# Turning a convolution filter to step-major: transposing DMAs and a DRAM bounce in place of identity matmuls

## The chip, the cores and the metric

The kernel runs on one core of one Trainium2 chip. The metric is the device time of one execution in microseconds (us); the time of a version is the median over its runs.

The core has a matmul engine (TensorE; PE in the profile, its weight loads PEld), a vector engine (VectorE, DVE), an activation engine (ScalarE, ACT), a general one (GpSimd, POOL) and a synchronizing one (SyncE, SP) that here issues nearly all loads. Each engine works through its own instructions in program order and waits for the others by semaphores. Transfers run on 16 DMA engines that all queues share.

## The reference, cut to what matters

```python
xn = layernorm(q)                                   # (1, 2048, 640)
# A: gated long convolution, channel by channel
k_shift = sum over t of k_pad[:, t:t+S, :] * shift_k[:, 3-t]    # 4 taps
kv  = k_shift * v
kv_f = rfft(kv padded to 2S);  kf_f = rfft(ssm_k padded to 2S)  # ssm_k: (640, 2048)
y   = irfft(kv_f * kf_f)[:2048] + kv * ssm_D
s   = xn * y
# B: a dense layer pair on the same xn
g   = silu(gelu(xn @ w1 + b1) @ w2 + b2)            # 640 -> 1728 -> 640
out = q + s * g
```

S is 2048 steps, D is 640 channels. All tensors are bfloat16. The filter `ssm_k` comes channel-major, one row of 2048 steps for each of 640 channels, while k, v and q come step-major.

## The kernel before, in words

The convolution is a discrete Fourier transform in two stages of matmuls. A step s is written as s = 16 p + n, with p one of 128 partitions and n one of 16. The first stage multiplies, for each n, a 128 x 640 slab (128 values of p by 640 channels) with two 128 x 128 matrices, WA and WB. For the signal these are the steps `uf`, for the filter the steps `kf`. The results are cast out of PSUM (`ue`, `ke`) and written to DRAM scratch (`us` to scrU, `ks` to scrK); they are read back in another order (`ml`, `fl`) and go through a second stage with small matrices (`mu`, `ff`). The filter's spectrum stays in the tile Khat; the signal's is multiplied with it (`mp`), and two inverse stages (`mc`, `y`) with another bounce through scrC give y. The dense pair B (`h` for the first layer, `g` for the second) works on four chunks of 512 steps, and its matmuls are laid between those of the convolution.

The order of all work is written out by hand: PLAN is a string of steps, and each step issues its instructions on the engines that it uses, so the order of steps is the order on each engine's queue. A suffix .a or .d says whether ACT or DVE does an evacuation.

The part that concerns us is how the filter gets from channel-major to the slabs that `kf` reads:

- `C0` to `C4` (load_kf, line 198, SP's queue) load 128 channels by 2048 steps each into the first 16 rows of Khat, seen as `kf_sb` (partition = channel within a tile of 128).
- `d` (add_d, line 498, DVE) adds ssm_D to step 0. This makes the skip term kv * ssm_D a part of the filter. ssm_D comes with the bias rows in `prm` (`P2`), is turned with them (`pt`, `pb`) and lies in `dD_sb` with the channel on the partition.
- `kt0` to `kt15` (k_tr, line 424, PE) turn, for each n, five 128 x 128 blocks by matmuls with the identity into one PSUM tile; `kc0` to `kc15` (k_tr_out, line 427, on ACT or DVE by the suffix, printed as L135 and L136) copy it to a row tile kT.
- `kf0` to `kf31` (k_f1, line 430 by way of mm2 at line 340, PE) multiply kT with WA and WB.

PSUM has three tiles of the kind "big" in turn; kt, kf, uf and the other convolution stages all use them. There are two row tiles for kT. The shifted and gated signal is made by `cv` steps on DVE; the step cv7 of the first pair of n multiplies with v's first quarter (`V0`), cv23 with the second (`V1`). Each `X` loads a chunk of q, each `K` a quarter of k. On POOL the queue holds the stores `ks`, `us`, `ms` and the small power `lr` (ln_root, line 359), which the normalization steps `ln` on DVE wait for.

Of the kernel before, what the change touches and what calls it, by code (L numbers as in the profile page):

```python
# [11 lines left out]
BF16 = mybir.dt.bfloat16  # L12
I32 = mybir.dt.int32
ACT = mybir.ActivationFunctionType
ALU = mybir.AluOpType

P = 128
S = 2048
D = 640
F = 1728  # L20
NJ = 16
DT = D // P
FT = (F + P - 1) // P
# [9 lines left out]
X1 ls4 ls5 ls7 ls6 lv1 C0 X3 cv17 cv18 g0 ge0 gm0 g1 ge1 gm1 ws0 cv19 g2 ge2 g3 ge3 g4 cv20 cv21 cv22 ws1 g5 lr1  # L33
ln7 ln5 ws2 C4 C3 C1 V0 cv7 cv15 C2 d kt0 kc0.a kt1 kc1.a kf0 kf1 ke0.a kt2 kc2.a V1 ln4 kf2 ke2.a cv24 cv23 X2
cv25 ke1.d ks0 gm2 ge4 ln6 kf3 ke3.d ks1 kf4 ke4.a gm4 ge5 kt3 kc3.d kf5 ke5.a ks2 V2 tt7 te7.a kt5 kc5.d tt9
te9.a kt4 gm5 kf7 cv26 cv27 cv28 kf6 kc4.a ke6.a ke7.a ks3 g6 ge6 kf8 ke8.a kf9 ke9.d ks4 kf10 ke10.a K2 tt8
te8.a kt6 kc6.d kf11 ke11.a ks5 kt9 kc9.d gm3 kf12 ke12.a tt5 te5.d tt6 te6.a uf1 kt7 kf13 kc7.a ke13.a ks6 g7
ge7 ls12 uf0 ue0.a ue1.d us0 cv29 cv30 cv31 V3 h14 he14 kf14 ke14.d kf15 ke15.d ks7 h15 he15 kt8 kc8.d kf19 kf18
ke18.a ke19.d ks9 kt10 kc10.a cv32 cv33 cv34 cv35 cv36 kf16 ke16.a kt12 cv40 kf17 kc12.a ke17.a ks8 h16 he16 uf3
uf2 ue2.a ue3.a us1 h17 he17 kf21 kf20 ke20.a ke21.d ks10 kt11 kc11.a h18 he18 uf5 uf4 ue4.a ue5.d us2 kf22  # L40
ke22.d ls10 h19 he19 kt14 kf24 ke24.d sm kf23 kc14.a ke23.a ks11 h20 he20 kf25 ke25.d ks12 kt13 kc13.d kf28
ke28.a h21 he21 uf6 ue6.a kf29 ke29.a ks14 uf7 ue7.a us3 h22 he22 h23 he23 kf26 ke26.a gm7 cv37 cv38 cv41 cv42
cv39 kf27 ke27.a ks13 kt15 kc15.d kf30 ke30.a kf31 ke31.a ks15 fl0 fl1 fl2 h24 he24 fl4 uf10 ue10.a gm6 ls15 ls8
ls9 uf8 ue8.a ls14 uf11 ue11.a us5 h25 he25 h26 he26 uf14 ue14.a cv43 ls13 lv3 lr3 h27 he27 cv44 ls11 lv2 lr2
cv45 cv46 cv47 uf12 ue12.a uf9 ue9.a us4 fl3 uf15 ue15.a us7 g8 ge8 gm8 ln13 ln9 uf13 ue13.a us6 fl5 g9 ge9 ff3
fe3.a ln12 ff1 fe1.d ln10 ff2 fe2.a cv56 ff0 fe0.a cv48 cv49 cv50 ln8 uf21 uf20 ue20.a ue21.a us10 ff8 fe8.a
ln11 g10 ge10 uf16 ue16.a ff6 fe6.d gm9 ff9 fe9.a fl7 ff5 fe5.a ff7 fe7.a fl9 ff4 fe4.a fl8 uf17 ue17.a us8 g11
ge11 cv51 cv52 cv53 cv54 cv55 ff11 fe11.a ff10 fe10.a fl6 uf18 ue18.d uf19 ue19.a us9 fl11 uf26 ue26.a cv57 cv58
cv59 uf24 ue24.a uf27 ue27.a us13 uf25 ue25.a us12 fl12 ff16 fe16.d ff17 fe17.a fl15 ff12 fe12.a tt12 te12.a
ff14 fe14.a cv60 cv61 cv62 cv63 ff18 fe18.a ff15 fe15.a fl13 g12 ff19 fe19.a fl10 uf22 ue22.d ff13 fe13.a fl14  # L50
uf31 gm11 ge12 uf30 ue30.a ue31.d us15 ff23 fe23.d gm12 uf23 ue23.a us11 gm10 tt14 te14.d uf29 uf28 ue28.d
ue29.a us14 mk0 ml0 ml1 mk1 mk2 mk3 ml2 ml3 ml5 ml4 ff31 fe31.a tt13 te13.a tt10 te10.d it0 ie0.d ff27 fe27.d
ff25 fe25.d g13 ge13 gm13 g14 ge14 gm14 ff29 fe29.d ln14 ff28 fe28.a ff24 fe24.d g15 ge15 gm15 ff21 fe21.a tt11
te11.d ff22 fe22.a mu0 mp0 ff26 fe26.a ml7 h28 he28 mu2 mp2 ml10 ml8 mu1 mp1 mk4 mc0 me0.a h29 he29 ff30 fe30.a
mu3 mp3 mk5 ml12 h30 he30 ml11 mc2 me2.a mu4 mp4 mc1 me1.a ms0 mu5 mp5 mk6 h31 he31 ml6 ff20 fe20.a mc3 me3.a
ms1 ln15 mu6 mp6 mc4 me4.a mu7 mp7 mk7 ml9 h32 he32 mu8 mp8 mc5 me5.a ms2 mc6 me6.a mu11 mp11 mc7 me7.a ms3 mu10
mp10 h33 he33 mu9 mp9 mk8 mk9 mc8 me8.a mc10 me10.a mu12 mp12 mu13 mp13 mk10 mc11 me11.a ms5 ml14 h34 he34 ml15
mc12 me12.a it1 ie1.d mc13 me13.a ms6 mu15 mp15 h35 he35 mu14 mp14 mk11 ml13 mc9 me9.a ms4 mu18 mp18 h36 he36
mc14 me14.a mu17 mp17 h37 he37 mu16 mp16 mk12 mc15 me15.a mu20 mp20 h38 he38 mu19 mp19 mk13 mc18 me18.a h39 he39
mu21 mp21 mk14 mc16 me16.a tt17 mc19 me19.a ms9 mc17 me17.a ms8 mu23 mp23 mc20 me20.a mu22 mp22 mk15 h40 he40  # L60
mc21 me21.a ms10 mu24 mp24 mu25 mp25 mc22 me22.a h41 he41 te17.d mc24 me24.a mu26 mp26 mc25 me25.a ms12 tt15
te15.a mu27 mp27 tt16 te16.d mc23 me23.a ms11 mc26 me26.a tt18 te18.d mu29 mp29 it3 ie3.a mu28 mp28 g16 ge16
gm16 mc27 me27.a ms13 it2 ie2.d tt19 te19.a mu31 mp31 mu30 mp30 ms7 q0 g17 ge17 gm17 mc28 me28.a mc31 mc29
me29.d ms14 mc30 me30.d me31.d ms15 yl5 yl2 yl0 yl4 yl3 yl1 yl6 yl11 yl15 q1 g18 ge18 gm18 g19 ge19 gm19 g20
ge20 gm20 g21 ge21 gm21 g22 ge22 gm22 g23 ge23 gm23 h42 he42 h43 he43 y0 yt0 yo0 h44 he44 h45 he45 h46 he46 y5
yt5 yl8 y4 yt4 yo4 yo5 ys2 y1 yt1 yo1 ys0 y3 yt3 h47 he47 h48 he48 h49 he49 h50 he50 h51 he51 y2 yt2 yl7 yl14
yl9 yl10 yl12 yo2 yo3 ys1 q2 h52 he52 h53 he53 h54 he54 h55 he55 y6 yt6 yl13 yo6 y7 yt7 yo7 ys3 q3 y8 yt8 yo8
y11 yt11 g24 ge24 g25 ge25 g26 y12 yt12 gm24 ge26 gm25 ga24 ga25 gs25 y15 yt15 g27 ge27 y14 yt14 y13 yt13 gm26
ga26 gm27 ga27 gs27 y9 yt9 yo9 ys4 y10 yt10 yo10 yo11 ys5 g28 ge28 gm28 ga28 g29 ge29 gm29 ga29 g30 ge30 gm30
ga30 gs30 g31 ge31 gm31 ga31 gs29 gs31  # L70
# [4 lines left out]
def kernel(  # L75
# [15 lines left out]
    nc = tc.nc  # L91
# [4 lines left out]
    NG = 32  # L96
# [7 lines left out]
    consts = ctx.enter_context(tc.tile_pool(name="consts", bufs=1))  # L104
    wts = ctx.enter_context(tc.tile_pool(name="wts", bufs=1))
    dram = ctx.enter_context(tc.tile_pool(name="dram", bufs=1, space=bass.MemoryType.DRAM))
# [11 lines left out]
    scrU = dram.tile([P * 32, D], BF16, name="scrU")  # L118
    scrC = dram.tile([P * 32, D], BF16, name="scrC")
# [13 lines left out]
    def evac(eng, out_ap, in_ap):  # L133
        if eng == "a":
            return nc.scalar.copy(out=out_ap, in_=in_ap)  # L135
        return nc.vector.tensor_copy(out=out_ap, in_=in_ap)  # L136
# [4 lines left out]
    Khat = wts.tile([P, NG + NR, D], BF16, name="Khat")  # L141
    skp = consts.tile([P, DT, 4], BF16, name="skp")
    prm = consts.tile([FT + DT, P], BF16, name="prm")
    b1_f = consts.tile([P, FT], F32, name="b1_f")
    dD_sb = consts.tile([P, DT], BF16, name="dD_sb")
    ident = consts.tile([P, P], BF16, name="ident")
# [5 lines left out]
    WA = consts.tile([P, NJ, P], BF16, name="WA")  # L152
# [28 lines left out]
    kf_sb = Khat[:, 0:NG // 2, :].rearrange("p g d -> p (g d)").rearrange("p (t j) -> p t j", t=DT)  # L181
    kf_v = kf_sb.rearrange("p t (a b) -> p t b a", b=NJ)

    def load_params(i):
        with nc.allow_non_contiguous_dma(reason="tiny parameter loads"):
            if i == 0:
                nc.sync.dma_start(out=prm[0:FT - 1, :], in_=B_b1[0:(FT - 1) * P].rearrange("(t p) -> t p", p=P))
            elif i == 1:
                nc.sync.dma_start(out=prm[FT - 1:FT, 0:FLAST], in_=B_b1[(FT - 1) * P:F].rearrange("(o p) -> o p", o=1))
            else:  # L190
                nc.sync.dma_start(out=prm[FT:FT + DT, :], in_=A_ssm_D.rearrange("(t p) -> t p", p=P))
# [4 lines left out]

    def load_kf(t):
        nc.sync.dma_start(out=kf_sb[:, t, :], in_=A_ssm_k[t * P:(t + 1) * P, :])
# [47 lines left out]
    sm = {}  # L246
# [68 lines left out]
    live = {}  # L315
# [7 lines left out]
    def big_of(key, bf=False):  # L323
        return take(key, ps_big, [P, 1024] if bf else [P, 2, 512], BF16 if bf else F32, "big")
# [4 lines left out]
    def row_of(key):  # L329
        return take(key, ep, [P, D], BF16, "row", NROW)  # L330
# [7 lines left out]
    def mm2(ps, lhsT, rhs, start=True, stop=True):  # L338
        for h in range(2):
            nc.tensor.matmul(out=ps[:, h, 0:HALF], lhsT=lhsT, rhs=rhs[:, h * HALF:(h + 1) * HALF], start=start, stop=stop)  # L340
# [80 lines left out]
    def k_tr(n2):  # L421
        tp = big_of(("kt", n2), True)
        for t in range(DT):
            nc.tensor.transpose(out=tp[:, t * P:(t + 1) * P], in_=kf_v[:, t, n2, :], identity=ident[:])

    def k_tr_out(n2, eng):
        evac(eng, row_of(("kT", n2))[:], live["kt", n2][:, 0:D])

    def k_f1(i):
        mm2(big_of(("kf", i)), (WA, WB)[i % 2][:, i // 2, :], live["kT", i // 2])  # L430
# [66 lines left out]
    def add_d():  # L497
        nc.vector.tensor_tensor(out=kf_sb[:, :, 0], in0=kf_sb[:, :, 0], in1=dD_sb[:], op=ALU.add)
# [7 lines left out]
    def param_tr():  # L506
        pt = big_of(("pt", 0), True)
        nc.tensor.transpose(out=pt[:, 0:FT + DT], in_=prm[:, :], identity=ident[0:FT + DT, 0:FT + DT])

    def param_out():  # L510
        pt = live["pt", 0]
        nc.vector.tensor_copy(out=b1_f[:], in_=pt[:, 0:FT])
        nc.vector.tensor_copy(out=dD_sb[:], in_=pt[:, FT:FT + DT])
# [59 lines left out]
    def prologue():  # L573
# [90 lines left out]
        "P": load_params, "pt": param_tr, "pb": param_out, "X": load_x, "A": load_w1, "B": load_w2, "C": load_kf, "K": load_k, "V": load_v,  # L664
# [4 lines left out]
        "kt": k_tr, "kc": k_tr_out, "kf": k_f1, "ke": k_f1_out, "ks": k_store,  # L669
# [40 lines left out]
```

## Time and profile before

| | |
|---|---|
| runs | 229.15, 231.75, 233.93 us; median 231.75 |
| the profiled execution, its span | 231.0 us |
| instructions | 3921 |
| DMA | 57.61 MB, mean 249 GB/s; HBM read 33.76 MB, written 18.35 MB |
| `kt` matmuls | 80, first at 42.7, last at 76.7 us |
| loads of ssm_k | 5 of 512 KB, issued from 16.0 to 24.9 us, landing 8.8 to 13.7 us later |
| stores to scrK | 16 of 320 KB, landing after 2.6 us (median) |
| loads from scrK | 16 of 320 KB, 4.6 us |

The profile is of one execution. Its span is 0.75 us below the median of the runs. Its page gives each engine's busy time and then the span in 40 slices of 5.8 us, where a digit is the busy share in tenths; PEclk is the clock granted to TensorE, DMA the mean busy share of the 16 DMA engines, GB/s what they moved. A listing by time has start, length, engine, line and operation, with "out<-in" by the names of the program, and in brackets the idle time before it and what ended it. "SPq" lines are DMA issues on SP's queue. For a DMA issue the last number is the time from issue to landing.

### The profile page before, as it was taken

The numbers are of one execution on the slowest core, as the hardware profiler recorded it, in microseconds if no ns is written. First come the engines' busy times: TensorE is split into PE (matmuls) and PEld (weight loads), VectorE is DVE, ScalarE is ACT, GpSimd is POOL, SyncE is SP. The second block draws the span as 40 slices with busy tenths as digits, with TensorE's granted clock in tenths as the row PEclk, the third lists the DMA queues.
The fourth block names the chain that finished last, engine by engine and source line by source line (L and its number), as shares of the span: only waits on it lengthen the run. The fifth ranks groups of instructions, "written<-read, shape, count | busy, mean of one in ns | idle before, by whom it ended". The sixth has DMA issues, their size and how long they took to land.

```text
span 231.0 us, 3921 instructions
## 1 busy us (share of the span) xinstructions
PE 211.6 (92%) x1420; PEld 131.7 (57%) x1420; DVE 184.1 (80%) x315; ACT 149.6 (65%) x232; POOL 43.1 (19%) x75
## 2 busy tenths in 40 slices
PE   7859999899999899979999965999999999999993
PEld 4524456677555556646765532556677765457772
DVE  7799999889989999999779885699998115444892
ACT  3934687998988999898468742567782244562111
POOL 8100020042232344120200220212222000100010
PEclk9988999999999999999999997999999999999999
DMA  7999995654844479599779999877943695379323
GB/s 219 349 380 355 409 413 206 191 209 174 305 191 188 179 236 381 176 309 337 266 215 294 303 353 295 257 231 188 270 156 131 207 340 200 150 218 367 124 89 114
DMA packets 25209, 57.61 MB, mean 249 GB/s; under 512 B 2854, under 2 KB 14055, under 8 KB 25190
## 3 DMA queue, kind: packets, MB, share of 16 engines
q1 hardware_dynamic: 20726, 39.66, 52.6%
q0 software_dynamic: 4320, 17.70, 20.5%
q8 instruction: 11, 0.18, 0.3%
q14 instruction: 8, 0.07, 0.1%
q10 hardware_dynamic: 144, 0.01, 0.0%
HBM read 33.76 MB, written 18.35 MB: 226 GB/s over the span
## 4 chain that ended last, share of the span: by engine, by line
PE 65%; ACT 12%; DMA 9%; DVE 8%; issue 3%; SPq 1%; DVEq 0%; ACTq 0%
PE g L399 22%; PE h L380 21%; ACT Khat L135 6%; DMA kh<-scrU 6%; PE uf L340 3%; PE mc L537 3%; DMA Khat<-Khat 3%; PE mc L538 2%; PE mu L340 2%; PE kf L340 2%; PE ff L340 2%; PE y L556 2%; PE y L557 2%; DMA skp<-in_A_shift_k_dram 1%; ACT sl L404 1%
## 5 line engine op out<-in xcount | busy, mean ns | idle before, releaser
L380 PE MATMUL h<-xnT,w_sb 128*128 128x512 bf16 x280 | 68.4, 390 | 1.5 <-ACT hT L386 1.2
L399 PE MATMUL g<-w_sb,hT 128*128 128x320 bf16 x448 | 63.7, 299 | 0.6 <-ACT sl L404 0.6
L386 ACT ACTIVATE hT<-h,b_f 128x512 bf16<-128x512 f32 (+1 forms) x56 | 38.3, 690 | 27.3 <-PE h L380 24.2
L399 PEld LDWEIGHTS <-hT 128*128 128x128 bf16 x448 | 43.8, 98 | 18.1 <-issue 0.8
L529 DVE TENSOR_TENSOR p<-mu,Khat 128x1280 bf16<-128x1280 f32 x32 | 45.8, 1484 | 5.4 <-PE mu L340 3.7
L380 PEld LDWEIGHTS <-w_sb 128*128 128x128 bf16 x280 | 27.9, 100 | 31.3 <-issue 4.6
L404 ACT ACTIVATE sl<-g 128x320 bf16<-128x320 f32 x32 | 13.9, 439 | 36.1 <-PE g L399 32.5
L135 ACT CAST c<-mc 128x640 bf16<-128x640 f32 x29 | 19.9, 692 | 8.6 <-PE mc L538 7.9
L544 POOL DMA_DIRECT2D scrC<-c x16 | 11.5, 718 | 56.0 <-ACT c L135 51.8
L409 DVE TENSOR_TENSOR xn<-xn,sl 128x320 bf16<-128x320 bf16 x32 | 10.1, 322 | 14.0 <-ACT sl L404 13.8
L472 DVE TENSOR_TENSOR uc<-uc,kvtmp 128x1280 bf16<-128x1280 bf16 x24 | 19.8, 824 | 0.7
L476 DVE TENSOR_TENSOR kvtmp<-kh,w_exp 128x1280 bf16<-128x1280 bf16 x24 | 19.7, 820 | 0.5
L340 PEld LDWEIGHTS <-mats 128*128 128x128 bf16 x128 | 12.1, 97 | 13.8 <-issue 4.9
L537 PE MATMUL mc<-p,mats 128*128 128x320 bf16 x64 | 18.6, 305 | 1.2 <-DVE p L529 0.7
L538 PE MATMUL mc<-p,mats 128*128 128x320 bf16 x64 | 18.5, 304 | 0.0
L563 DVE TENSOR_TENSOR t<-y,xn 128x640 bf16<-128x640 f32 x12 | 9.8, 820 | 10.4 <-PE y L557 10.3
L135 ACT CAST Khat<-uf 128x640 bf16<-128x640 f32 x26 | 17.0, 697 | 0.4 <-PE uf L340 0.4
L340 PE MATMUL mu<-kh,mats 128*128 128x320 bf16 x64 | 13.5, 300 | 3.7 <-DMA kh<-scrU 2.5
L135 ACT CAST Khat<-ff 128x640 bf16<-128x640 f32 x24 | 15.5, 699 | 0.5 <-PE ff L340 0.4
L135 ACT CAST Khat<-kf 128x640 bf16<-128x640 f32 x22 | 15.1, 711 | 0.3 <-PE kf L340 0.2
L440 POOL DMA_DIRECT2D scrK<-Khat x16 | 8.9, 554 | 31.2 <-ACT Khat L135 16.6
L340 PE MATMUL ff<-kin,mats 128*128 128x320 bf16 x64 | 12.3, 298 | 1.4 <-ACT Khat L135 1.3
(111 smaller groups left out, 269.4 us busy)
## 6 DMA issues: line engine op xcount, KB each, us to landing
scrK<-Khat POOLq DMA_DIRECT2D x16, 320.0 KB, 2.6
scrU<-Khat POOLq DMA_DIRECT2D x16, 320.0 KB, 4.2
kin<-scrK SPq DMA_DIRECT2D x16, 320.0 KB, 4.6
Khat<-Khat SPq DMA_DIRECT2D x32, 160.0 KB, 4.2
kh<-scrU SPq DMA_DIRECT2D x16, 320.0 KB, 5.4
scrC<-c POOLq DMA_DIRECT2D x16, 320.0 KB, 3.9
kh<-scrC SPq DMA_DIRECT2D x16, 320.0 KB, 6.2
kh<-in_A_k_dram SPq DMA_DIRECT2D x4, 640.0 KB, 6.1
```

What stands on the lines that cost most here:

```text
L135: return nc.scalar.copy(out=out_ap, in_=in_ap)
L340: nc.tensor.matmul(out=ps[:, h, 0:HALF], lhsT=lhsT, rhs=rhs[:, h * HALF:(h + 1) * HALF], start=start, stop=stop)
L380: nc.tensor.matmul(out=ps[:, :], lhsT=w1_sb[:, t, ft * P:(ft + 1) * P], rhs=xnT[:, t, :], start=(t == 0), stop=(t == DT - 1))
L386: nc.scalar.activation(out=hT[0:M, ft, :], in_=live["h", i][0:M, :], func=ACT.Gelu_apprx_tanh, bias=b1_f[0:M, ft:ft + 1], scale=1.0)
L399: nc.tensor.matmul(out=ps[:, 0:HALF], lhsT=hT[0:M, ft, q * P:(q + 1) * P], rhs=w2_sb[0:M, ft, hs], start=(ft == 0), stop=(ft == FT - 1))
L404: nc.scalar.activation(out=sl[:], in_=live["g", i][:, 0:HALF], func=ACT.Silu)
L472: nc.vector.tensor_tensor(out=uc[:], in0=uc[:], in1=kvtmp[:], op=ALU.add)
L476: nc.vector.tensor_tensor(out=(kvtmp if s else uc)[:], in0=kh[:, r0:r0 + KC, :], in1=w_exp[:, j:j + 1, :].to_broadcast([P, KC, D]), op=ALU ...
L529: nc.vector.tensor_tensor(out=p[:].rearrange("p k (h c) -> p k h c", h=2), in0=live["mu", g][:, None, :, 0:HALF].to_broadcast([P, 2, 2, HA ...
L537: nc.tensor.matmul(out=psC[:, h, 0:HALF], lhsT=I1a, rhs=p[:, 0, hs], start=True, stop=False)
L538: nc.tensor.matmul(out=psC[:, h, 0:HALF], lhsT=I1b, rhs=p[:, 1, hs], start=False, stop=True)
L544: nc.gpsimd.dma_start(out=pair_view(scrC)[g2], in_=live["c", g2][:])
```

## The change

The filter is turned by the DMA engines. Four transposing loads (`C0` to `C3`) each read 512 steps of all 640 channels from DRAM and write them to four rows of Khat with the step within a block of 128 on the partition: Khat[q, j] holds step 128 j + q. That is step-major, but with the step split as 128 j + q and not as 16 p + n. So four stores (`cb0` to `cb3`, POOL's queue) write these rows to a DRAM scratch scrT in the order of steps, and four loads (`cl0` to `cl3`, SP's queue, 32 partitions each) read it back as s = 16 p + n into the same rows of Khat. `kf` then reads Khat in place of kT; the steps `kt` and `kc` are gone. ssm_D is loaded as a row of 640 (`P2`), and `d` adds it to partition 0 of Khat's row 0; dD_sb and its five rows of prm are gone.

```diff
+    scrT = dram.tile([S, D], BF16, name="scrT")
...
-    prm = consts.tile([FT + DT, P], BF16, name="prm")
+    prm = consts.tile([FT, P], BF16, name="prm")
-    dD_sb = consts.tile([P, DT], BF16, name="dD_sb")
...
-    kf_sb = Khat[:, 0:NG // 2, :].rearrange("p g d -> p (g d)").rearrange("p (t j) -> p t j", t=DT)
-    kf_v = kf_sb.rearrange("p t (a b) -> p t b a", b=NJ)
+    def turn_k(i):
+        nc.sync.dma_start_transpose(out=Khat[:, 4 * i:4 * i + 4, :], in_=A_ssm_k[:, 4 * i * P:4 * (i + 1) * P])
+
+    def bounce_k(i):
+        nc.gpsimd.dma_start(out=scrT.rearrange("(j q) d -> q j d", q=P)[:, 4 * i:4 * i + 4, :], in_=Khat[:, 4 * i:4 * i + 4, :])
+
+    def load_kT(i):
+        a, b = i * 32, i * 32 + 32
+        nc.sync.dma_start(out=Khat[a:b, 0:NJ, :], in_=scrT.rearrange("(p n) d -> p n d", n=NJ)[a:b])
...
-                nc.sync.dma_start(out=prm[FT:FT + DT, :], in_=A_ssm_D.rearrange("(t p) -> t p", p=P))
+                nc.sync.dma_start(out=row_of(("D", 0))[0:1, :], in_=A_ssm_D.rearrange("(o d) -> o d", o=1))
...
-    def load_kf(t):
-        nc.sync.dma_start(out=kf_sb[:, t, :], in_=A_ssm_k[t * P:(t + 1) * P, :])
...
-    def k_tr(n2):
-        tp = big_of(("kt", n2), True)
-        for t in range(DT):
-            nc.tensor.transpose(out=tp[:, t * P:(t + 1) * P], in_=kf_v[:, t, n2, :], identity=ident[:])
-
-    def k_tr_out(n2, eng):
-        evac(eng, row_of(("kT", n2))[:], live["kt", n2][:, 0:D])
-
     def k_f1(i):
-        mm2(big_of(("kf", i)), (WA, WB)[i % 2][:, i // 2, :], live["kT", i // 2])
+        mm2(big_of(("kf", i)), (WA, WB)[i % 2][:, i // 2, :], Khat[:, i // 2, :])
...
     def add_d():
-        nc.vector.tensor_tensor(out=kf_sb[:, :, 0], in0=kf_sb[:, :, 0], in1=dD_sb[:], op=ALU.add)
+        row = Khat[0:1, 0, :]
+        nc.vector.tensor_tensor(out=row, in0=row, in1=live["D", 0][0:1, :], op=ALU.add)
...
     def param_tr():
         pt = big_of(("pt", 0), True)
-        nc.tensor.transpose(out=pt[:, 0:FT + DT], in_=prm[:, :], identity=ident[0:FT + DT, 0:FT + DT])
+        nc.tensor.transpose(out=pt[:, 0:FT], in_=prm[:, :], identity=ident[0:FT, 0:FT])
...
     def param_out():
         pt = live["pt", 0]
         nc.vector.tensor_copy(out=b1_f[:], in_=pt[:, 0:FT])
-        nc.vector.tensor_copy(out=dD_sb[:], in_=pt[:, FT:FT + DT])
```

In PLAN the order around the filter's loads becomes this, and apart from it only the `kt` and `kc` steps are taken out:

```text
before: K1 cv16 X1 ls4 ls5 ls7 ls6 lv1 C0 X3 cv17 cv18 g0 ... g4 cv20 cv21 cv22 ws1 g5 lr1 ln7 ln5 ws2
        C4 C3 C1 V0 cv7 cv15 C2 d kt0 kc0.a kt1 kc1.a kf0 kf1 ke0.a kt2 kc2.a V1 ln4 kf2 ke2.a cv24 cv23 X2 cv25 ke1.d
after:  K1 cv16 X1 ls4 C0 cb0 ls5 ls7 ls6 lv1 X3 C1 cb1 C2 cb2 C3 cb3 cv17 cv18 g0 ... g4 cv20 cv21 cv22 ws1 g5 lr1
        cl0 cl1 ln7 ln5 ws2 V0 cl2 cl3 cv7 cv15 d kf0 kf1 ke0.a V1 ln4 kf2 ke2.a cv24 cv23 X2 cv25 ke1.d
```

## The prediction

> **What bounds the kernel now.** I read the page's head first, then the stretches of six microseconds, then the instructions of each engine in order of time around the filter work, then the DMA issues.
>
> ```profile
> PE 211.6 (92%) x1420; PEld 131.7 (57%) x1420; DVE 184.1 (80%) x315; ACT 149.6 (65%) x232; POOL 43.1 (19%) x75
> ...
> DMA  7999995654844479599779999877943695379323
> GB/s 219 349 380 355 409 413 206 191 209 174 305 191 188 179 236 381 176 309 337 266 215 294 303 353 295 257 231 188 270 156 131 207 340 200 150 218 367 124 89 114
> ```
>
> TensorE is busy in 92% of the span and its program is one fixed order, so a wait at one place moves all that follows. The DMA engines are full in the first six slices (35 us), idle right after, and never full for long again. The filter lies at that seam:
>
> ```profile
> 16.00:17.00 1.00, 0.95 (x3) 0.39 (x3) 1.00 (x3) 0.58 (x1) 0.00 (x0) 0.50 1.07 362
> ...
> 30.00:36.00 6.00, 5.36 (x38) 3.61 (x37) 5.51 (x15) 5.55 (x8) 1.55 (x1) 1.00 1.03 415
> 36.00:42.00 6.00, 6.00 (x46) 4.30 (x44) 5.90 (x11) 4.50 (x5) 0.00 (x0) 1.00 0.27 108
> 42.00:48.00 6.00, 5.11 (x51) 3.91 (x49) 4.67 (x9) 5.99 (x10) 1.17 (x2) 1.00 0.81 250
> ...
> 84.00:90.00 6.00, 5.71 (x43) 3.97 (x42) 5.86 (x13) 5.84 (x10) 4.63 (x5) 1.00 1.02 352
> ```
>
> Columns: stretch and length, busy time of PE, PEld, DVE, ACT, POOL, then granted clock, DMA share and GB/s. At 30 to 36 full DMA engines move 415 GB/s; from 36 to 42 they are nearly free while PE, DVE and ACT are full. From 42 on ACT is the fullest.
>
> ```profile
> 35.08 7.78 PE L399 MATMUL g<-w_sb,hT 128*128 128x320 bf16 x56 [0.64 <-ACT sl L404]
> 42.70 0.78 PE L424 MATMUL kt<-ident,Khat 128*128 128x128 bf16 x10
> 44.08 0.43 PE L340 MATMUL kf<-kT,WA 128*128 128x320 bf16 x2 [0.60 <-ACT kT L135]
> ```
>
> TensorE reaches the filter at 42.7 us and the first kf runs at 44.1. All it needs from DRAM landed some 5 us before: the filter costs no wait today. The inputs come by SP's queue in this order:
>
> ```profile
> 15.51 0.43 SPq L168 DMA_DIRECT2D xn<-in_A_q_dram  x1
> 15.98 0.43 SPq L198 DMA_DIRECT2D Khat<-in_A_ssm_k_dram  x1
> 16.46 0.43 SPq L168 DMA_DIRECT2D xn<-in_A_q_dram  x1
> 16.93 6.94 SPq L198 DMA_DIRECT2D Khat<-in_A_ssm_k_dram  x3
> 23.91 0.43 SPq L179 DMA_DIRECT2D vc<-in_A_v_dram  x1
> ...
> xn<-in_A_q_dram SPq DMA_DIRECT2D x1, 640.0 KB, 11.0
> ```
>
> The last line is the issue at 15.51 (chunk 1 of x, X1): it landed at 15.51 + 11.0 = 26.5. Issued behind it in the same queue, the filter's bytes move after 26.5 in both kernels.
>
> **What is removed.** 80 transposes and 16 copies.
>
> ```profile
> L135 ACT COPY kT<-kt x9: 672/693/785, 43.4 to 70.2; 128x640 bf16<-128x640 bf16 x9
> L136 DVE COPY kT<-kt x7: 481/492/492, 47.2 to 77.1; 128x640 bf16<-128x640 bf16 x7
> ...
> 59.96 0.31 PE kt L424 x5
> ```
>
> In the chain of waits (start, length, what) five transposes take 0.31, so PE loses 16 x 0.31 = 5.0 us; ACT 9 x 0.69 = 6.2; DVE 7 x 0.45 (0.49 less overlap) = 3.1. In the six stretches from 42 to 78 the busy sums are PE 33.9, ACT 33.8, DVE 32.7 of 36; afterwards 28.9, 27.6, 29.6. No engine can then need less than 29.6, so the gain is at most 6.4, at least some 3 if waits between the engines stay; I take 5.0, PE's own share. Edits in the parameter transpose and add_d (0.15 to 0.2 us each) count nothing: they lie beside DVE's wait, below.
>
> **What is added: a chain of DMAs in front of the first kf.** The filter is 2048 x 640 x 2 = 2.62 MB. Before, it was moved once; now three times (turned in, written out, read back), and each pass must be complete before the last starts: every kf reads all 128 partitions, which come by four loads, and each load overwrites rows of Khat that all four stores still read. Step by step:
>
> 1. *Four transposing loads, 0.655 MB each.* No row shows one. Lower bound: 415 GB/s, 1.6 us. Upper: pieces of 256 bytes (128 columns), 10240 in all, each at a price per packet from the page's two big queues (20726 packets of 1913 bytes at 93.8 ns, 4320 of 4097 bytes at 175 ns, by share times 16 engines times span): 37 ps per byte plus 23 ns, so 32 ns, over 16 engines 20.6 us, 5.2 each. Nearest row: reading runs of 1024 bytes is like the loads from scrK with 1280-byte rows, 352 GB/s at 84 to 90, hence 1.9; I take 2.4 for the finer writing. The Trainium skill (DMA: Bandwidth & Descriptors, Latency and other measured facts) has one measured DMA transpose at 261 GB/s, which would be 2.5 us each and 0.4 us more in all; no run shows it yet.
> 2. *The stores (cb), 0.655 MB each, on POOL's queue.* cb0 to cb2 run beside the later transposes but on the same engines: 1.6 each. So C0 lands at 26.5 + 2.4 = 28.9, X3 (1.6) at 30.5, C1 at 30.5 + 2.4 + 1.6 = 34.5, C2 38.5, C3 42.5. cb3 is exposed: issue 0.55 (the scrK stores' 0.54), landing 2.6 for 320 KB plus 0.8 for the second half: 46.45.
> 3. *The loads (cl) with V0 among them.* A lone 640 KB load of v took 4.2 us at the least, 1.6 of them bytes: 2.6 fixed. V0 1.6. The four loads fill 32 partitions each: at full rate 6.4; at that of the stretch below, where the swaps between partition halves are in flight and full DMA engines (1.04) move only 250 GB/s, 10.5. So 10.6 to 14.7, near neither; 12.5. Last load at 59.0.
>
> ```profile
> 120.00:124.00 4.00, 4.00 (x24) 2.25 (x23) 3.60 (x3) 3.97 (x7) 0.00 (x0) 1.00 1.04 250
> ```
>
> First kf at 59.0 instead of 44.1: 14.9 later, PE idle from 42.7. Nothing covers this: everything behind kf0 on PE waits with it. After such an idle time the granted clock falls: at 16 to 19 us, after PE's gaps from 13.5, it is 0.50 for 3.4 us. That costs up to 1.7; I take 1.5. PE's sum: 14.9 + 1.5 - 5.0 = +11.4.
>
> *Who else waits.* POOL's stores stand ahead of ln_root for chunk 1 (lr1), which waits until C3 lands: 42.5 + 0.55 + 1.55 = 44.6 instead of 34.8; DVE's ln7, ln5 wait with it, but DVE's next, cv7, needs V0, now at some 53, so that is hidden. SP's V1 stands behind the four loads: 59.0 + 1.6 = 60.6. DVE's cv23, which uses it, ran at 42.3: 18.3 later, and ke1 and the kf buffers queue behind it. Of this DVE recovers its idle time (36 - 32.7 = 3.3) and its copies (3.1): 18.3 - 6.4 = +11.9. X2, V2 and K2 are needed well after.
>
> The larger of the two, 11.9, moves the end: everything after 84 us waits only for engines or for DMAs that this chain itself feeds, so nothing takes it back. 231.0 + 11.9 = 242.9 for the span of the profiled execution; the median of the runs stands 0.3% above that span (231.75), so **243.7**.
>
> **Bounds.** Least: after 26.5, 4 transposes, X3, 4 stores, 4 loads and V0 are 9.2 MB; at 415 GB/s 22.1 us, plus some 3 for the two hand-overs: 51.6, 7.5 late; less 6.4, plus 1: +2.1, some 234. Most: 5.2 per transpose (C3 at 53.7, cb3 at 57.7) and loads at 14.7: 72.4, 28.3 late, less 3, plus 1.7: +27, some 259.
>
> **Rivals.**
> - *Faster (0.04).* The place is the wait of the first kf on the last load; if the filter is there by 42.7, PE's 5.0 is pure gain, 226.7. It pays from readiness before 44.5, since 2% is 4.6 us. For: the DMA engines idle from 36 to 42. Against: 9.2 MB in a dependent chain from 26.5 gives 51.6 even at the best rate in the page.
> - *No change within 2% (0.13).* The chain runs near the best rate and the removed work returns 6.4: 233.5 to 236.4. For: full DMA engines do hold 415 GB/s for 6 us. Against: the half-partition slices, and that stores and transposes share engines.
> - *A dear transpose (0.18).* By pieces of 256 bytes, with slow loads: 251 to 259. For: the packet fit; against: it prices reading runs that are four times as long.
> - *Tiles one after another (0.05).* If the 80 blocks of 128 x 128 (32.8 KB) went through one after another, each at one engine's rate (415 / 16 = 26 GB/s, 1.26 us), the transposes would take 101 us, C3 would land at 129, the last load at 145, and with +101 late, +1.5, -5 the sum would be some 329. No transfer in the trace is confined so, nor is any a transpose. The Trainium skill (VectorE: DVE Perf Modes, The three transpose paths) gives 1309 ns for a 128 x 128 block by DMA against 390 on TensorE and advises TensorE where its output may go to PSUM; here the trace has a TensorE block at 62 ns in a row.
> - *Not a turning DMA at all (0.02).* If it became copies of single elements, 1.31 million pieces at 23 ns over 16 engines are 1.9 ms.
> - *My forecast (0.58):* 237 to 251.
>
> **How the numbers follow.** A measurement of this kernel tells about 2% from no change. Faster 0.04; within 2% 0.13 (227.1 to 236.4); slower the rest, 0.83. The range 234 to 256 leaves out the faster case (0.04), the last two rivals (0.07) and the ends of the unchanged (0.02) and the dear one (0.07), 0.2 together.
>
> **What would show it.** Khat's transposing issues landing 2 to 3 us apart from 29 on, the last at 42 or so; stores to scrT ending near 46; the four loads ending near 59; PE idle from 42.7 until then with its first kf at a granted clock of 0.5; DVE idle before its product with vc; no kt group; and the order of work after the first kf a little denser than before. I am wrong if the first kf starts before 51 (the chain is cheaper than its bytes), if PE finds other work in the gap, if a later wait gives back the delay, or if a single transpose takes over 5 us.

## The result and the profile after

| | before | after |
|---|---|---|
| runs, median (range) | 230.89 us (229.15 to 233.93, 4 runs) | 257.92 us (255.40 to 258.62, 4 runs) |
| ratio of after to before, 95% interval | | 1.1185, 1.1081 to 1.1289 |
| profiled execution, its span | 231.0 us | 255.3 us |
| DMA moved; packets, of these under 512 bytes | 57.61 MB; 25209, 2854 | 62.83 MB; 35615, 13261 |

The kernel before has one run more here (230.04) than in the table ahead of the prediction. Some executions of a kernel are 1 to 2% longer than others without any change; the ratios leave these out, the medians and the spans do not.

The changed kernel is slower by 12%: 24.3 us of span. The head of its page:

```profile
PE 209.2 (82%) x1340; PEld 126.7 (50%) x1340; DVE 181.1 (71%) x307; ACT 144.3 (57%) x223; POOL 45.4 (18%) x79
...
PEclk9979999555579999999999999979999999999999
DMA  6999999589963855696995899979693469359422
GB/s 218 365 376 343 180 303 321 184 179 257 334 252 150 298 205 205 207 344 221 306 328 194 234 334 317 346 207 304 166 275 149 156 216 368 125 183 347 165 77 103
```

TensorE is busy for 2.4 us less in all (211.6 before), although its span is 24 us longer: time was added in which it does nothing. The seam that the forecast looked at, in stretches of six microseconds (stretch and length, busy time of PE, PEld, DVE, ACT, POOL, granted clock, DMA share, GB/s):

```profile
36.00:42.00 6.00, 6.00 (x46) 4.29 (x45) 2.55 (x4) 4.50 (x5) 1.52 (x2) 1.00 1.13 270
42.00:48.00 6.00, 0.48 (x4) 0.11 (x2) 0.80 (x2) 1.07 (x1) 1.82 (x2) 0.82 0.80 283
48.00:54.00 6.00, 0.00 (x0) 0.00 (x0) 0.00 (x0) 0.00 (x0) 0.00 (x0) 0.50 0.77 175
54.00:60.00 6.00, 0.00 (x0) 0.00 (x0) 0.00 (x0) 0.00 (x0) 0.00 (x0) 0.50 1.07 246
60.00:66.00 6.00, 0.00 (x0) 0.00 (x0) 3.04 (x5) 0.00 (x0) 0.00 (x0) 0.50 0.88 192
```

From 42 to 66 the compute engines stand nearly still while the DMA engines are busy at 175 to 283 GB/s, not at 415. TensorE's listing names what the first kf waited for (start, length, and in brackets the idle time and what ended it):

```profile
37.83 4.66 PE L402 MATMUL g<-w_sb,hT 128*128 128x320 bf16 x33
66.42 0.69 PE L343 MATMUL kf<-Khat,WA 128*128 128x320 bf16 x2 [23.94 <-DMA Khat<-scrT]
```

The whole path is in the chain of waits (start, length, what):

```profile
16.36 11.93 SPq L181
...
28.33 0.57 SPq L167
...
28.95 5.17 SPq L181
...
37.32 7.40 DMA Khat<-in_A_ssm_k_dram
...
45.00 3.66 DMA scrT<-Khat
...
51.52 16.26 DMA vc<-in_A_v_dram
```

L181 is the transposing issue. The first held SP's queue for 11.93 us; the last, C3, landed at 44.72; the last store, cb3, at 48.66; then come four read-back loads with V0, and behind them V1, which took 16.26 us to land at 67.78. This last step is the one on DVE's path: its product with V1 (cv23) ran at 67.87, 25.6 us later than before (42.29). In DVE's listings, before and then after:

```profile
42.29 0.82 DVE L470 TENSOR_TENSOR uc<-uc,vc 128x1280 bf16<-128x1280 bf16 x1
```

```profile
67.87 0.83 DVE L465 TENSOR_TENSOR uc<-uc,vc 128x1280 bf16<-128x1280 bf16 x1 [4.74 <-DMA vc<-in_A_v_dram]
```

The same matmul can be timed in both kernels, since the order on TensorE is the same but for the kt group. The first kf is 22.3 us late (66.42 against 44.08), kf8 25.9, kf23 23.8, ff18 23.4, the first y 24.0, the last 24.0. So the loss arises in front of kf8; 2.2 us come back by kf23, where the kt and kc steps are missing, and nothing in the 150 us that follow.

### The profile page after: what moved, and what is told of

Read it like the earlier page. It is cut to its first block, busy times and chain, and to the rows that moved or that the text cites. A ratio compares the mean times of both kernels' runs of the same rounds, so it can differ in the third digit from the quotient of the medians.

```text
span 255.3 us, 3757 instructions
## 1 busy us (share of the span) xinstructions
PE 209.2 (82%) x1340; PEld 126.7 (50%) x1340; DVE 181.1 (71%) x307; ACT 144.3 (57%) x223; POOL 45.4 (18%) x79
## 2 busy tenths in 40 slices
DMA packets 35615, 62.83 MB, mean 246 GB/s; under 512 B 13261, under 2 KB 24463, under 8 KB 35470
## 4 chain that ended last, share of the span: by engine, by line
PE 41%; DMA 25%; SPq 13%; DVE 11%; ACT 4%; issue 4%; POOL 0%; DVEq 0%; POOLq 0%; ACTq 0%
PE g L402 16%; PE h L383 11%; SPq L181 8%; DMA vc<-in_A_v_dram 6%; DMA scrU<-Khat 5%; DMA kh<-scrU 4%; ACT Khat L135 3%; DMA Khat<-in_A_ssm_k_dram 3%; PE mc L532 3%; DVE Khat L136 3%; PE mu L343 2%; DMA kh<-in_A_k_dram 2%; PE mc L533 2%; SPq L205 2%; DVE st L353 2%
## 5 line engine op out<-in xcount | busy, mean ns | idle before, releaser
L383 PE MATMUL h<-xnT,w_sb 128*128 128x512 bf16 x280 | 67.6, 388 | 1.3 <-ACT hT L389 1.0
L402 PE MATMUL g<-w_sb,hT 128*128 128x320 bf16 x448 | 65.3, 304 | 0.8 <-ACT sl L407 0.6
L343 PE MATMUL kf<-Khat,WA 128*128 128x320 bf16 x32 | 7.6, 328 | 24.4 <-DMA Khat<-scrT 23.9
L539 POOL DMA_DIRECT2D scrC<-c x16 | 11.4, 715 | 56.6 <-ACT c L135 52.4
L343 PEld LDWEIGHTS <-WA 128*128 128x128 bf16 x64 | 6.3, 100 | 29.9 <-issue 26.1
L412 DVE TENSOR_TENSOR xn<-xn,sl 128x320 bf16<-128x320 bf16 x32 | 10.1, 322 | 14.2 <-ACT sl L407 14.0
L465 DVE TENSOR_TENSOR uc<-uc,vc 128x1280 bf16<-128x1280 bf16 x8 | 6.5, 824 | 17.3 <-DMA vc<-in_A_v_dram 17.2
L558 DVE TENSOR_TENSOR t<-y,xn 128x640 bf16<-128x640 f32 x12 | 9.8, 821 | 10.6 <-PE y L552 10.5
```

The costliest lines, as they stand in the source:

```text
L383: nc.tensor.matmul(out=ps[:, :], lhsT=w1_sb[:, t, ft * P:(ft + 1) * P], rhs=xnT[:, t, :], start=(t == 0), stop=(t == DT - 1))
L402: nc.tensor.matmul(out=ps[:, 0:HALF], lhsT=hT[0:M, ft, q * P:(q + 1) * P], rhs=w2_sb[0:M, ft, hs], start=(ft == 0), stop=(ft == FT - 1))
```

## The experiments

Twelve kernels were run. A ratio is to the kernel before, timed on the same chip; "late" is how much later a matmul starts than in the trace of before, both from the start of the span. The experiments ran on four chips, on which the kernel before has medians of 231.2 to 233.6 us, so ratios compare better than times, and a span, which is one execution's, tells no difference of a us or so. For the changed kernel the ratio is 1.1185, the first kf at 66.42 and the span 255.3.

**1. Read-back over all partitions.** Same bytes, but each load fills 4 rows of all 128 partitions, not 16 rows of 32.

```diff
-        a, b = i * 32, i * 32 + 32
-        nc.sync.dma_start(out=Khat[a:b, 0:NJ, :], in_=scrT.rearrange("(p n) d -> p n d", n=NJ)[a:b])
+        a, b = i * 4, i * 4 + 4
+        nc.sync.dma_start(out=Khat[:, a:b, :], in_=scrT.rearrange("(p n) d -> p n d", n=NJ)[:, a:b, :])
```

> The four loads of the read-back are cut by rows instead of partitions: each fills all 128 partitions of four rows of Khat, with the same bytes, the same order and the same waits. In the changed kernel they took 17.5 us from the first issue (48.9) to the first kf (66.4). Theory (a load confined to 32 partitions goes at about half the rate): the last load lands at 57 to 59; the first kf then waits for the step that adds D, which stands on DVE behind the product with the first quarter of v, some 58 to 60; span 246 to 249. Rival (the loads are slow because v and x stand between and behind them on the same engines): the same bytes take the same time, first kf at 65 to 66.5, span 254 to 256.

251.11 us, ratio 1.0824 [1.0735, 1.0912], span 248.6, first kf 57.66, which now waits for DVE's add of D behind its product with V0: the theory. In two-microsecond stretches, first the changed kernel while its loads run, then this one:

```profile
50.00:52.00 2.00, 0.00 (x0) 0.00 (x0) 0.00 (x0) 0.00 (x0) 0.00 (x0) 0.50 0.96 215
52.00:54.00 2.00, 0.00 (x0) 0.00 (x0) 0.00 (x0) 0.00 (x0) 0.00 (x0) 0.50 0.92 184
54.00:56.00 2.00, 0.00 (x0) 0.00 (x0) 0.00 (x0) 0.00 (x0) 0.00 (x0) 0.50 0.86 174
```

```profile
52.00:54.00 2.00, 0.00 (x0) 0.10 (x1) 0.00 (x0) 0.00 (x0) 0.00 (x0) 0.50 1.02 422
54.00:56.00 2.00, 0.00 (x0) 0.00 (x0) 0.34 (x1) 0.00 (x0) 0.00 (x0) 0.50 1.01 420
```

The last two columns are what matters: engines nearly equally busy, but 174 to 215 GB/s against 420. The page shows the engines "busy" in both; only the bytes tell that a load into 32 partitions goes at half the rate. In the span it costs 6.7 us of the 24.3.

**2. v ahead of the last store.** V0, V1 and X2 issued right behind C3.

```diff
-C3 cb3 ... ws2 V0 cl2 cl3 cv7 cv15 d kf0 kf1 ke0.a V1 ln4 kf2 ke2.a cv24 cv23 X2
+C3 V0 V1 X2 cb3 ... ws2 cl2 cl3 cv7 cv15 d kf0 kf1 ke0.a ln4 kf2 ke2.a cv24 cv23
```

> V0, V1 and X2 are issued right after the last transposing load, ahead of the four loads of the read-back. Theory (DVE, held by V1 until 67.9, sets the delay of 26 us at the ninth kf): DVE's product with V1 runs before 58, the delay behind the first kf is no longer above that of the first kf itself, which comes at 65 to 67; span 251 to 254. Rival (the slow clock after the idle time sets it): the delay still grows by 3 to 4 us from the first to the ninth kf; span 254 to 256.

258.49 us, 1.1069 [1.0939, 1.1199], span 256.2: no gain, and outside both ranges. The loads were issued at 54.35, 5.5 later, because v's bytes now stand in front of them; the first kf ran at 69.29. But its delay hardly grows: 25.2 late at kf0, 25.7 at kf8, against 22.3 and 25.9. DVE's products with v were done by 62.2 here; in the changed kernel they run where TensorE restarts and stand ahead of the kf evacuations. A part of that kernel's growth of 3.6 us lies in the 14 matmuls of g just ahead of kf8, first in the changed kernel, then here:

```profile
73.31 3.67 PE L402 MATMUL g<-w_sb,hT 128*128 128x320 bf16 x14
```

```profile
74.72 2.07 PE L402 MATMUL g<-w_sb,hT 128*128 128x320 bf16 x14
```

In the changed kernel the granted clock was back at 1.00 from 69.8 on and fell to 0.50 again from 73.2 to 76.6, under these matmuls. Here it was 0.50 up to 74.5 and 1.00 from then on. So 1.6 of the 3.6 us are matmuls at half clock, and 2.0 come before them, where TensorE waits for DVE and ACT and the first kf run at half clock as well. TensorE was busy for only 1.6 of the 3 us from 70 to 73; that these waits brought on the second fall of the clock is likely, but not shown.

**3. TensorE kept warm.** 105 matmuls of 512 columns whose result nobody reads, in front of the first kf.

```diff
+    def keep_warm():
+        pw2 = big_of(("wm", 0))
+        for _ in range(105):
+            nc.tensor.matmul(out=pw2[:, 0, :].rearrange("p (a b) -> p a b", a=4), lhsT=ident[:],
+                             rhs=ident[:, None, :].to_broadcast([P, 4, P]), start=True, stop=True)
```

> 105 matmuls on the identity (some 23 us at 0.216 us each, on a PSUM tile that nobody reads) fill TensorE's idle time ahead of the first kf. Theory (the half clock costs 2 to 4 us): the granted clock is 1.0 from 66 to 78, the first kf pairs take 0.43 us and not 0.7, the 14 matmuls of g after them 2.1 and not 3.7; span 251.5 to 253.5. Rival (DVE's late V1 paces that stretch): clock as said, but the span stays at 254.5 to 256.

261.21 us, 1.1238 [1.1156, 1.132]: a miss. The added matmuls ended at 64.55, but C3 landed only by 49.76 in this execution, the first kf came at 70.86, after 6.31 idle, and its granted clock was down to 0.50 again. So the run says nothing on the clock. Why C3 was later is open (more on that at the end).

**4. Removal alone.** The kernel before without kt and kc, and kf reading the unturned Khat: the filter is not turned, no DMA is added.

```diff
-        mm2(big_of(("kf", i)), (WA, WB)[i % 2][:, i // 2, :], live["kT", i // 2])
+        mm2(big_of(("kf", i)), (WA, WB)[i % 2][:, i // 2, :], Khat[:, i // 2, :])
```

> The kernel before with the 80 transposes and their 16 copies left out: kf reads the filter's rows as they were loaded, unturned. It measures what the removal alone is worth, with no added DMA. Forecast: TensorE's share of 5.0 us, 225.5 to 226.5 for the span. Rival (the stretch from 44 to 78 us is paced by evacuations on ACT and DVE that stay, or the removed work filled waits): 2 to 3 us, 228 to 229.

231.82 us (10 runs) against 231.24 (13 runs), ratio 1.0023 [0.9976, 1.007]. In the profiled execution (span 228.5, the rival's figure) the lead was 2.1 us by kf23, 2.8 by ff18 and 2.5 at the end; over the runs it is nothing. The 80 transposes and 16 copies, 5.0 us of TensorE, 6.2 of ACT and 3.1 of DVE, were worth 2.5 us between two traces and nothing over the runs.

**5. Plain loads in place of the turning ones.** Same bytes into the same rows, unturned.

```diff
-        nc.sync.dma_start_transpose(out=Khat[:, 4 * i:4 * i + 4, :], in_=A_ssm_k[:, 4 * i * P:4 * (i + 1) * P])
+        flat = A_ssm_k.rearrange("(p r) s -> p (r s)", p=P).rearrange("p (j d) -> p j d", d=D)
+        nc.sync.dma_start(out=Khat[:, 4 * i:4 * i + 4, :], in_=flat[:, 4 * i:4 * i + 4, :])
```

> The four transposing loads are replaced by plain loads of the same bytes into the same rows of Khat (5120 contiguous bytes per partition, nothing turned); stores, read-back and waits stay. Theory (turning is dear in itself: 18 ns for each 256-byte packet, 10240 of them, 2.9 us per load against 1.6): the last of the four lands 4 to 6 us earlier than in the changed kernel (45.0), at 39 to 41; first kf at 60 to 62; span 249 to 252. Rival (the transposes cost about what their bytes cost, the rest of the chain sets the time): landing at 43 to 45, span 253.5 to 256.

249.43 us, 1.0729 [1.0649, 1.0808], span 246.9, first kf 58.02. POOL's stores show when each quarter has landed; the last of them, in the changed kernel and then in this one:

```profile
45.00 0.75 POOL L184 DMA_DIRECT2D scrT<-Khat  x1 [4.14 <-DMA Khat<-in_A_ssm_k_dram]
```

```profile
35.81 0.75 POOL L185 DMA_DIRECT2D scrT<-Khat  x1 [2.13 <-DMA Khat<-in_A_ssm_k_dram]
```

Turning costs 9.2 us over the four loads, more than the theory's 4 to 6; the plain loads have 5120 contiguous bytes a partition, so the finer pieces are a part of it. The packet records come near it: those of 256 bytes add up to 15.8 us over 16 engines, 512 of 5120 bytes at 201 ns to 6.4. SP's queue is held too: the first issue takes 11.93 us when it transposes and 0.43 when it is plain, so X3 and C1 are issued at 16.81 and 17.28 in place of 28.33 and 28.95. How much of the 9.2 that makes, no run separates:

```profile
16.33 0.43 SPq L182 DMA_DIRECT2D Khat<-in_A_ssm_k_dram  x1
16.81 0.43 SPq L167 DMA_DIRECT2D xn<-in_A_q_dram  x1
17.28 6.42 SPq L182 DMA_DIRECT2D Khat<-in_A_ssm_k_dram  x3
```

**6. No bounce.** The steps cb and cl left out: the filter is turned but keeps the split 128 j + q.

> Stores to scrT and the read-back are left out: kf reads the rows as the transposing loads leave them, with the steps in the other order. Theory (the bounce makes most of the delay): the first kf waits for V0 and the step that adds D, some 45 to 48, and the span is 231 to 236. Rival (the transposes and what they push back, V0 and V1, make most of it): first kf after 52, span above 240.

236.68 us, 1.0176 [1.0083, 1.027], span 235.2; the first kf at 45.97, behind DVE's product with V0 and the add of D, not behind the filter:

```profile
45.97 0.69 PE L305 MATMUL kf<-Khat,WA 128*128 128x320 bf16 x2 [4.19 <-DVE Khat L456]
```

So the bounce makes some 20 us of the 24.3 (255.3 - 235.2). With the 8.4 of experiment 5 that is more than the whole: the two are not shares of one sum, and a part of the turn's cost shows only when the bounce stands behind it. Even with a bounce that cost nothing, the kernel would be no faster than before.

**7. Order.** Experiment 1 with ln_root early, d ahead of cv7, and V0 and V1 right behind cl0.

```diff
-g5 lr1 cl0 cl1 ln7 ln5 ws2 V0 cl2 cl3 cv7 cv15 d kf0 kf1 ke0.a V1 ...
+g5 cl0 V0 V1 cl1 cl2 cl3 X2 ln7 ln5 ln4 ws2 d cv7 cv15 kf0 kf1 ke0.a ...
```

> On top of the loads over all partitions (span 248.6): ln_root of chunk 1 goes ahead of the second store on POOL, V0 and V1 go right behind the first of the four loads and X2 behind the last, and the step that adds D goes ahead of the products with v. Theory (the first kf needs only the first load, and DVE is held by V0 and V1): first load lands at 52 to 53, first kf at 53 to 54.5 instead of 57.7, DVE's product with V1 at 57 to 59 instead of 61.7; span 244 to 246. Rival (the stretch after it is paced by something else, so an earlier start is lost): 247.5 or more.

249.04 us, 1.0684 [1.0597, 1.0771], span 246.9. The first kf came at 54.67, 3.0 us before that of experiment 1, but the end only 1.7 earlier, between the theory's range and the rival's: 10.6 late at kf0, 16.6 at kf8, 15.5 at the last y. The products with v now stand behind the add, just where TensorE restarts.

**8. TensorE's gap filled.** Experiment 7 with the rest of chunk 1's normalization, its transposes (tt5 to tt9), g6, g7 and h14 to h27 moved ahead of the first kf.

> As e7, and TensorE's idle time is filled with work of the same kernel that needs no filter: chunk 1's normalization, its turning, the last two products of chunk 0 (g6, g7) and chunk 1's first layer (h14 to h27), 20.4 us of matmuls, moved ahead of the first kf with their evacuations; the filter's and the signal's steps keep their order behind it. Theory (the delay costs because nothing stood in its way): the first kf is no longer waited for, it runs at 62 to 65, and the span comes down to 232 to 238. Rival (the moved matmuls were cover for evacuations and loads later, whose waits now show): 240 to 245.

251.89 us, 1.0792 [1.0702, 1.0883]; span 251.8 in the profiled execution, the longest of its four. The gap was full, the first kf ran at 67.78, and the end came no earlier, later even than the rival's 240 to 245. Behind it DVE showed 5.8 to 5.9 of 6 us busy from 78 to 114, which made DVE the suspect for the next two.

**9. DVE's gap filled.** Experiment 7 with fourteen of DVE's later products (cv24 to cv30, cv32 to cv38) moved into its idle time, and cv23 and cv31 ahead of the first kf.

```diff
-C3 cb3 ... ln5 ln4 ws2 d cv7 cv15 kf0 kf1 ke0.a kf2 ke2.a cv24 ke1.d
+C3 cb3 K2 V0 ... ln5 ln4 ws2 cv24 cv25 cv26 cv27 cv28 cv29 cv30 cv32 cv33 cv34 cv35 cv36 cv37 cv38 d cv7 cv15 cv23 cv31 kf0 kf1 ke0.a kf2 ke2.a ke1.d
```

> e7_order with twelve to twenty of VectorE's later products (cv24 to cv30, cv32 to cv38, cv40 to cv46, with K2 and V0 issued earlier for them) moved into VectorE's idle time ahead of the first kf; TensorE's order is unchanged. Theory: behind the gap VectorE is what all wait for (5.8 to 5.9 of 6 us busy in e8_gap_filled), and its idle time in the gap (about 10 us in e7_order) is what the kernel never gets back; then the first kf stays at 54 to 57 us and the span falls from 246.9 to 236 to 242. Rival: TensorE's own order behind the first kf, or ScalarE's evacuations, set the pace; then the delay against the kernel before stays at 15 us or so and the span at 245 or more.

249.73 us (six runs, 247.65 to 254.05), 1.0749 [1.0625, 1.0873], span 245.9: the rival. The stretches of this kernel show where the moved work went missing:

```profile
42.00:54.00 12.00, 0.25 (x2) 0.00 (x0) 10.16 (x13) 0.83 (x1) 0.75 (x1) 0.68 0.88 304
78.00:84.00 6.00, 5.67 (x32) 3.22 (x33) 1.43 (x3) 5.51 (x10) 2.33 (x5) 1.00 0.56 220
96.00:102.00 6.00, 6.00 (x40) 3.69 (x39) 0.62 (x1) 5.81 (x9) 3.70 (x5) 1.00 0.75 240
```

DVE (third busy column) did 10.16 us in the gap, none in experiment 7, and then idles at 78 and at 96 (5.52 and 5.78 there in experiment 7), while PE and ACT stay full. DVE's busy time was not the bound.

**10. Both filled.** Experiment 8 with the same products moved.

> e8_gap_filled (TensorE's dense work for chunk 1 moved ahead of the first kf) with the same products of VectorE moved there too. Theory: in e8_gap_filled TensorE's gap was full but VectorE's was not, so the end came no earlier; with both full the span falls from 251.8 to 231 to 240. Rival: the dense matmuls are missed as cover later, whatever VectorE does; then the span stays at 244 or more.

250.39 us, 1.0714 [1.0544, 1.0885], span 251.5 in the profiled execution, the longest of its four: the rival again. TensorE's listing behind the first kf shows what the dense work is missed for:

```profile
72.37 0.43 PE L342 MATMUL kf<-Khat,WB 128*128 128x320 bf16 x2 [0.51 <-ACT Khat L134]
72.97 0.43 PE L342 MATMUL kf<-Khat,WA 128*128 128x320 bf16 x2 [0.16 <-ACT Khat L134]
75.16 0.43 PE L342 MATMUL kf<-Khat,WB 128*128 128x320 bf16 x2 [1.76 <-ACT Khat L134]
```

A kf takes 0.43 and its evacuation on ACT 0.69; without h or g matmuls between them, TensorE waits for ACT. From the first kf to ff3 it idles for 9.5 us, some 7 of them until ACT is done, against 1.5 before; so 20.4 us of matmuls moved out of this stretch bring the lateness down by only 9.2, from 23.5 to 14.3. By the first y it is back at 20.1; why, no run was made to find. Work moved into the gap is paid for later.

**11. Read-back by halves.** Four loads of 64 partitions and 8 rows.

```diff
-        a, b = i * 32, i * 32 + 32
+        a, b, j = i // 2 * 64, i // 2 * 64 + 64, i % 2 * 8
```

> The changed kernel with its read-back in four loads of 64 partitions and 8 rows (partitions 0 to 63 twice, then 64 to 127 twice), in place of four of 32 partitions and 16 rows; the bytes are the same. Theory: half of the partitions are reached by half of the paths, so the loads still move some 200 GB/s (174 to 225 with 32 partitions, 415 to 422 with 128), the first kf starts at 65 to 67 us and the span stays near 255. Rival: the rate grows with the number of partitions or with the number of pieces, and 64 partitions already reach 400 GB/s or more; then the first kf starts at 58 to 60 us and the span is 247 to 250.

258.89 us, 1.1074 [1.0928, 1.1221]: not told apart from the changed kernel, well above experiment 1. The profiled execution (span 261.2, the longest of the four) has C3 landing late again, at 48.82, and its second load waits for cb3, so its first kf at 66.44 is not a clean reading. The trace's packet records are: median 798 ns for 10240 bytes, 13 bytes per ns; 1605 ns for the 20480 of the changed kernel, also 13; 196 ns for the 5120 of experiment 1, 26. So 64 partitions get no more than 32, half of the rate of 128. The packets of the three loads differ in length as well, and no run separates that from the partitions. The Trainium skill (SBUF — State Buffer, Door 1: The DMA port swizzle) states this as a rule: what counts is how many of 16 ports the partitions of one load reach, and partitions 0 to 31 reach the same eight as 0 to 63; it gives 189 and 196 GB/s for the two, measured with 1 MiB. The trace agrees, with 13 bytes per ns in both, some 205 GB/s over 16 engines.

**12. Both sized terms at once.** Plain loads (the filter is not turned) and the read-back of experiment 1.

> The changed kernel with plain loads in place of the transposing ones (so the filter is not turned) and the read-back in four loads of 128 partitions by 4 rows; three passes over the filter's bytes remain, all at plain rates. Theory: the two costs that the forecast sized too low add up, since both stand in one chain; e1_all_partitions took 6.7 us and e5_plain_first_loads 8.4 us off the span of 255.3, so the first kf starts near 66.4 - 8.8 - 8.4 = 49 us and the span is near 255.3 - 15.1 = 240, which with V1 behind it is between the forecast's least case and its middle. Rival: v's second quarter (V1) or DVE's queue takes the place of the filter's last load, so the second saving is mostly lost and the span stays at 244 or more.

245.96 us, 1.0538 [1.0473, 1.0603], span 245.1, first kf 50.95. Up to ff18 the savings add: 10.3 late, where 23.4 less 6.3 (experiment 1) less 7.8 (experiment 5) makes 9.3. From there to the last y 3.5 us more are lost; the granted clock was 0.50 from 152 to 159, for 6.9 us, where experiment 1 has 3.4 us of it in this part (159 to 162) and experiment 5 none. That this made the loss was not tested. The span is in the rival's range (244 or more) and not at the theory's 240, though it is the longest of four (241.9 to 245.1). The rival had the wait right: the first kf waited for DVE, whose product with V0 stood ahead of the add of D until 50.4. But the second saving was not mostly lost. Three passes over the filter, all at plain rates, still cost 5%.

No version tried beats the kernel before. The best that still computes the filter's turn and order is experiment 7, 7% slower.

## Why the prediction was right or wrong

The direction and the mechanism were right: an exposed chain of DMAs in front of the first kf, with V1 behind it. The size was wrong: 243.7 forecast, 257.92 measured, 2 us above the range. The 14.2 us are 12.4 of span (255.3 against 242.9) and 1.8 of what lies around it: the median stood 2.6 above the profiled span, not 0.8. Of the 12.4, the turn makes 2.2, the loads with V0 5.2, and the recovery that did not come 5.1. Step by step:

| step | forecast | measured |
|---|---|---|
| C0, C1, C2 landed | 28.9, 34.5, 38.5 | by 30.5, 37.6, 40.1 |
| C3 landed | 42.5 | 44.72 |
| cb3 landed, after C3 | 46.45, 3.95 | 48.66, 3.94 |
| V0, four loads; first kf, after cb3 | 59.0, 12.55 | 66.42, 17.76 |
| V1 landed; cv23 later by | 60.6; 18.3 | 67.78; 25.6 |
| of this recovered | 6.4 | 1.3 |
| span later by | 11.9 | 24.3 |

- *The loads: the term that failed most.* V0 and four loads were put at 12.5 with 14.7 as the most; they took 17.8, 3.28 MB at 184 GB/s. The upper bound came from a stretch at 250 GB/s, the slowest with full DMA engines that was quoted. That stretch mixes swaps between partition halves with other traffic, so it was no bound for a load that is confined throughout. The Trainium skill's rule of the port swizzle, cited in experiment 11, was not drawn on; with the limit of 218 GB/s that it gives for eight ports, an estimate is 12.0 for the four loads, and with V0's 1.6 and the 2.6 of fixed time 16.2, near the 17.8 measured. Experiment 1 shows the term: 415 to 422 GB/s once all partitions are filled.
- *The recovery: the second.* It was said that DVE recovers 3.3 of idle time and 3.1 of its copies. Of 25.6 it recovered 1.3. Experiment 4 shows that the copies and transposes are worth 0 to 2.5 us even without the delay, and experiment 9 that DVE's free time is not what sets the end: 10 us of it, given back, moved the end by 1.0 in the span and nothing in the runs. The busy sums gave a floor for the stretch, 29.6 of 36 us; they did not say that the waits between the engines would shrink to it. The 5.0 taken off TensorE's sum had the same fault: 2.2 of it came back.
- *The transposes.* 2.4 each was too little: the trace's packet records show 10240 packets of 256 bytes at 18 ns (median), so 11.5 us over 16 engines, 2.9 each, 228 GB/s; with 132 much longer records among them it is 15.8 us, 4.0 each. The Trainium skill (DMA: Bandwidth & Descriptors, Latency and other measured facts) has 261 GB/s, 2.5 each; the trace is below that by either count. A term was left out beside it: a transposing issue holds SP's queue, so X3 and C1 started at 28.3 and later, not at 26.5. With both, C3 was 2.2 late against forecast, a small miss; against plain loads the turn costs 9.2 (experiment 5).
- *The half clock.* The forecast had 1.5 us in TensorE's sum. The clock did fall to 0.50, and a second time under the matmuls of g, which cost 1.6 (experiment 2). The same experiment shows that a restart at half clock adds only 0.5 us from kf0 to kf8 when DVE's products with v are out of the way. With its terms as measured TensorE's sum is 22.3 + 3.6 - 2.2 = 23.7, not 11.4, and so near the 24.0 at the end.
- *The hand-over and the order.* cb3's 3.95 held to 0.01. V1 behind the loads is on the chain of waits, as said, and is its last DMA ahead of the kf stage. That it alone sets the end is not shown: in experiment 2 it was out of the way, the first kf came 2.9 later, and kf8 came within 0.2 of the changed kernel's. lr1 was hidden as said: ln7 ran at 46.87, 8.22 idle, with DVE's next work not ready until 60.09.
- *Rivals.* The range of the dear transpose, 251 to 259, holds the result, but by luck: its price (5.2 each, C3 at 53.7) was not paid, and the slow loads, named in it as an addition, were the larger half. Tiles one after another (C3 at 129) is out: all four had landed by 44.72, so the 1309 ns per block of the Trainium skill (VectorE: DVE Perf Modes, The three transpose paths) is not a price to be multiplied by 80 here. The Trainium skill's advice, TensorE for such a turn (VectorE: DVE Perf Modes, Rules for kernel authors), agrees with the result, but the 12% are mostly the bounce and not the turn: without the bounce it is 1.8% (experiment 6).
- *What would show it.* Seen: Khat's issues before the first kf, TensorE idle from 42.48, granted clock 0.50 there, DVE's wait of 12.41 ahead of its product with V0, no kt group. Not seen: transposes 2 to 3 us apart (7.1, 2.5 and 4.9 between the stores that follow them). Seen in part: an order behind the first kf that is denser than before, by 2.2 us from kf8 to kf23, but only after 3.6 had been lost up to kf8.

## What to carry to other kernels

When a compute step is traded for transfers, cost the chain of them at the place where it must be complete: three passes over 2.62 MB came to 22 us of wait, while the work they saved was worth 0 to 2.5. Before a large load is split, look which axis the split leaves whole: a split by rows over all partitions kept the full rate, a split by partitions lost half of it, with the DMA engines shown as busy either way. Freed busy time is a gain only where a wait ends earlier by it; removing the step alone, with no replacement, is a cheap run that tells.

## What the runs showed of the hardware

- The read-back loads that fill 32 or 64 of the 128 partitions moved 13 bytes per ns in a packet, those over all of them 26; in stretches, 174 to 225 GB/s (32 partitions) against 415 to 422. Their packets differ in length too (20480, 10240 and 5120 bytes), which no run separates.
- The first transposing DMA issue held SP's queue for 10.2 to 11.9 us where a plain one of the same size at the same place took 0.43; everything issued behind it on that queue waited. The next three took 3.1 to 5.2 us each.
- A 256-byte packet of the transposing loads took 18 ns (median; with the few long ones, 25 on average), less than the 32 ns that a line through the page's two big queues gave.
- C3's landing differs between executions whose DMA program is the same up to there: the store behind it was issued at 44.15 in experiment 1 and at 45.00 in the changed kernel, but at 49.10 and 49.76 in experiments 11 and 3. No run was made to find the cause; it stays open. In experiment 3 it is no stray execution: its four runs (259.87 to 262.48 us) are all longer than all four of the changed kernel.
